# A state-space layer's first transform: half of the shift of its rows added by VectorE in the copy out of PSUM, and a new placing of the first stage's jobs and buffers

## The chip, the core and the metric

The kernel runs on one core of a Trainium2 chip. A core has five engines, each with its own queue of instructions that it takes in order: TensorE (PE in the profile; PEld is its weight load), VectorE (DVE), ScalarE (ACT), GpSimd (POOL) and SyncE (SP), which here only issues DMAs. TensorE writes PSUM; VectorE and ScalarE read and write PSUM and SBUF; GpSimd works on SBUF. The metric is the device time of one execution in microseconds.

## What is computed

A row of 2048 tokens with 640 channels passes a modulated layer norm, a long convolution whose filter comes from 192 complex modes per channel (an S4 layer), a second modulated layer norm and a bilinear gated unit.

```python
    mod = (_silu(c) @ w_mod).reshape(c.shape[0], 6, 1, -1)
    sa, ca, ga, sb, cb, gb = (mod[:, i] for i in range(6))
    h = _layernorm(x, axis=-1) * (1 + ca) + sa
    x = x + ga * _A_ref(h, ...)      # y = irfft(rfft(h) * rfft(K)) + h * Dskip
    h = _layernorm(x, axis=-1) * (1 + cb) + sb
    x = x + gb * _B_ref(h, ...)      # ((h @ w_gate) * (h @ w_up)) @ w_down
...
    P = jnp.exp(logdA[:, :, None] * l[None, None, :])
    K = jnp.einsum("dn,dnl,dn->dl", Cc, P, dB).real
```

## The kernel before, in words

The work falls into two stages. The **first stage** is the convolution. It takes the channels in five blocks of 128 (`db` 0 to 4). The **second stage** (the gated unit, from `u_head` on) is a fixed sequence of large matmuls.

The spine of the first stage is a loop of 40 filter steps (`n`, eight to a block), each in three parts (`t` = 3n, 3n+1, 3n+2). A step makes the modes' powers for 16 channels: GpSimd makes phases `Ph` and magnitudes `EQ` and `EP` as outer sums and products (line 729), ScalarE takes sines into PSUM tiles `tr`, VectorE multiplies them into `QtA`, `PtA`, `PtB`, `QtB` (lines 784, 785, 790, 810), and TensorE multiplies those into the filter `kg` (lines 825 and 840), which ScalarE copies to `Kt`.

All other work of the first stage consists of **jobs** that are hung between the parts of the steps:

- `u_seeds` (lines 524 to 680) prepares a block's modes, with exponentials on ScalarE; `tab_ph` makes tables on GpSimd.
- `u_stats` and `u_hm` normalise the input rows and store them to `hm` in DRAM; `u_modr`, `u_modc`, `u_modg` and `u_fold` compute the modulation (line 368 is its product), and `u_fold` leaves the shift of each channel, the same on every partition, in `shr`.
- `u_pre(db, q)`, 20 in all, is the first transform of the rows: it loads a tile `hf` from `hm`, multiplies it by the constants `t_s1h` (line 886) into two PSUM banks, `r[0]` for the real and `r[1]` for the imaginary half, adds the transform of the constant shift by a product of a constant row `t_one` with `shr` (one partition deep) into the same banks, and copies both banks to `hf` tiles, which are stored to `FH`.
- `u_k` transforms the filter (line 862), `u_g` and `u_c` do the second transform (line 907, constants `t_tw`), the product of the two spectra on VectorE (lines 946 to 956) and the inverse (line 967, constants `t_ti`), whose result `W` is stored to `WD` in DRAM; `u_d` loads `WD` into `TV` and the input rows into `xs`, does the last inverse product (line 988), adds the rows and stores `x2d`.

Each job is a generator that runs in pieces. The table `SCHED` gives every piece a number; the pieces whose number divided by ten is x are issued, in the order of their numbers, at the call `due(x)`, and there are two such calls in each part of a step. So the table alone sets the order on every engine's queue, those of the DMA issuers included. Tiles come from small **rings**: the table `SLOT` names for every allocation which buffer it takes (`hfa`, `hfb`, `hfc`, `xsa`, `xsb`, the PSUM banks `psfa`, `psfb`, `psfc`, and so on), and a tile waits until the last use of the one before it in that buffer.

At the end of the first stage `u_d` of block 4 gives the last columns of each row; `u_head` takes the row statistics, normalises, transposes and begins the gated unit. `warm` matmuls fill TensorE meanwhile.

Of the kernel before, what the change touches and what calls it, by code (L numbers as in the profile page):

```python
# [10 lines left out]
F32 = mybir.dt.float32  # L11
# [20 lines left out]
    ml=(47, -888, -934),  # L32
    mr=(((138, 140), (110, 111)), ((2, 74), (4, 83)), ((0, 27), (-862, 18))),
    st=(
        (48, 91),
        (69, 100),
        (71, 101),
        (-948, 5),
        (-1006, 0),
        (-965, 89),  # L40
        (-1010, -969),
        (-868, 34),
        (-938, -874),
        (-918, 0),
        (-1003, -929),
        (-947, -909),
        (-919, -868),
        (34, 63),
        (37, 69),
        (-912, 0),  # L50
    ),
    hm=(
        (10, 220),
        (302, 416),
        (-1002, 172),
        (-999, 389),
        (-1010, 182),
        (-961, 147),
        (59, 100),
        (123, 173),  # L60
        (246, 310),
        (290, 372),
        (162, 252),
        (121, 180),
        (210, 293),
        (297, 381),
        (391, 486),
        (473, 556),
    ),
    rstd=(124, 87),  # L70
    tab=(367, 828),
    fo=(162, 162, 208, 238),
    e0=(4, 158),
    ds=(483, 468, 275, 262),
    mc=((87, 192, 194, 200, 210), (153, 286, 303, 326, 337), (270, 359, 369)),
    q=(
# [4 lines left out]
    ),  # L81
    pre=(
# [5 lines left out]
    ),  # L88
    c=(
# [4 lines left out]
        (  # L94
            (2433, 2608, 2608, 2648, 2679, 2703),
            (2425, 2484, 2537, 2554, 2645, 2677),
            (2477, 2493, 2636, 2656, 2680, 2719),
            (2387, 2439, 2532, 2545, 2620, 2633),
# [8 lines left out]
    ),  # L107
    k=(
        (392, 464),
        (371, 384),  # L110
        (474, 512),
        (494, 503),
        (622, 637),
        (592, 599),
        (710, 710),
        (607, 639),
        (640, 677),
        (652, 660),
        (831, 865),
        (797, 803),  # L120
        (973, 990),
        (941, 961),
        (1060, 1060),
        (1060, 1060),
        (1125, 1152),
        (1353, 1363),
        (1274, 1275),
        (1390, 1425),
        (1482, 1495),
        (1506, 1519),  # L130
        (1576, 1590),
        (1524, 1542),
        (1757, 1758),
        (1791, 1791),
        (1747, 1747),
        (1720, 1720),
        (2005, 2019),
        (1893, 1909),
        (2048, 2049),
        (2020, 2031),  # L140
        (2083, 2095),
        (2218, 2252),
        (2287, 2298),
        (2350, 2355),
        (2328, 2328),
        (2344, 2352),
        (2461, 2497),
        (2497, 2510),
    ),
    low=(168, 419, 677, 899, 1101, 1385, 1631, 1857, 2075),  # L150
    w=(2478, 2613, 2684, 2668, 2879, 2879),
    wl=(2590, 2441),
    wm=(2732, 2755),
    h=(2709, 2738, 2775, 2811, 2843, 2843, 2857, 2875),
    g=(
# [5 lines left out]
    ),  # L161
)

SLOT = dict(
    Kt="abababbaabababbababa",
    Ph="ababababababababababbbabababababaaababbb",
    PtA="abababababababababababababababbabaababba",
    TV="baabababaabbaabbbabbaababbaababbaabbabbaababab",
    W="abbbbbabababbbbabbaabbaba",
    f16="abababa",  # L170
    gh="cbacbacbcacbacbacbbcbcacbabccaabcabacba",
    hf="abacbcabacbacabcbacccacaabbcbaacabaabbabcaccababbcbbacaabcabbcbba",
    psf="cacabccbcaccbabbaacbbcacabacbcbacacbbaacabbcabcabcbacbbcbcbcababccbacabcabacbacbaccacbacbaccababbcabcabcabbcabcabcacacab"
    "cbcbaacbacbacbabccabcaacabcaabcbcabcabccabcabcbbacbcbacbacbacbacbacbbabccabacbaacbcabcbacabcabcabcabcababcacbabcacbaacbc"
    "abaabcabcacbacbacacbacbacaaacacbcaba",
    tr="bbababababababababababababababababababababababbabbabababaababbaaababababababababababababababababbbabbababaababababbabbbb"
    "a",
    xs="aabababbabaaabababab",
)
SEG0 = ("l", "a", "b", "c", "ud", "r", "x", "e", "f", "G", "g", "", "h", "v", "R", "")  # L180
SEG = ("l", "a", "b", "c", "ud", "r", "R", "x", "eE", "f", "g", "h", "v", "D")
P_PH, P_EP, P_MOD = 3, 6, 1


def _tables():

    a = np.arange(32)
# [42 lines left out]
def tile_kernel(ctx: ExitStack, tc: tile.TileContext, I, out):  # L230
# [3 lines left out]
    def act(o, i, f=AF.Copy, **kw):  # L234
        return S.activation(o, i, f, **kw)  # L235
# [1656 lines left out]
```

## Time and profile before

| | us |
|---|---|
| median of three runs | 965.52 (962.56 to 967.35) |
| the profiled execution, its own time | 962.34 |
| its span, first to last instruction | 960.6 |

The profile shows that one execution. Busy time is the time in which an engine executed instructions; a row of a group gives an instruction's line, engine, operation, output and inputs with their shapes, the number of them, the busy time in us and the mean duration in ns, then the idle time of the engine just before and what ended it. A row of the timeline gives start and duration in us; in square brackets stands how long the engine sat idle and who released it. TensorE's records of one product are two, one for each pass. The last columns of a row by stretches are the granted clock of TensorE (1.00 is full speed), the busy share of the DMA engines and GB/s.

### The profile page before, as it was taken

To read this page: it belongs to the slowest core of one execution; us is meant where nothing else is said; L and a number is where in the kernel's file an instruction comes from. 1 tells how busy PE (TensorE), PEld (TensorE's weight loads), DVE (VectorE), ACT (ScalarE), POOL (GpSimd) and SP (SyncE) were. 2 spreads that over 40 slices of the span, in tenths; PEclk is the share of its full clock that TensorE was granted. 3 is DMA by queue.
4 is the path that set the end of the run, shared out by engine and by line. 5 is a ranking of instruction groups with operands and counts; after the bars stand their busy time and mean duration, and the time that the engine had idled before them with its cause. 6 is when DMAs were issued, how large, how long until landed. Compare 5 with 4: busy or idle time off the path is not lost.

```text
span 960.6 us, 27559 instructions
## 1 busy us (share of the span) xinstructions
PE 892.6 (93%) x11646; PEld 734.0 (76%) x11646; DVE 705.6 (73%) x1250; ACT 580.5 (60%) x1016; POOL 471.2 (49%) x369
## 2 busy tenths in 40 slices
PE   1898787999899899998889999999999999999998
PEld 1675555878776677887558888889999788888997
DVE  8977888878888986767688555557585766569952
ACT  6989999887988977763276333234463543435430
POOL 3998997986699668750041345320013323231110
PEclk9989999999999999999999999999999999999999
DMA  7876546435267646547894675435536576758875
GB/s 238 324 243 242 186 131 199 146 108 153 78 207 197 187 124 194 184 128 228 277 308 152 192 246 192 165 140 172 200 120 196 171 238 208 244 172 289 253 231 189
DMA packets 158819, 188.59 MB, mean 196 GB/s; under 512 B 9828, under 2 KB 128360, under 8 KB 157544
## 3 DMA queue, kind: packets, MB, share of 16 engines
q1 hardware_dynamic: 149480, 155.51, 50.3%
q0 software_dynamic: 4752, 21.63, 7.8%
q10 hardware_dynamic: 4464, 9.70, 2.7%
q8 instruction: 91, 1.49, 0.6%
q14 instruction: 32, 0.26, 0.1%
HBM read 124.22 MB, written 62.59 MB: 194 GB/s over the span
## 4 chain that ended last, share of the span: by engine, by line
PE 61%; ACT 12%; issue 10%; DVE 7%; POOL 5%; DMA 4%; SPq 0%; POOLq 0%; DVEq 0%; ACTq 0%
PE pa L1095 19%; PE psg L1095 9%; PE pa L1527 7%; PE kg L825 3%; PE kg L840 2%; PE psfa L907 2%; PE psfb L967 2%; PE psfb L907 2%; ACT L235 2%; PE psfc L967 1%; PE psfc L907 1%; PE psfa L967 1%; PE psfc L886 1%; ACT trb L235 1%; ACT tra L235 1%
## 5 line engine op out<-in xcount | busy, mean ns | idle before, releaser
L1072 POOL TENSOR_TENSOR tf<-wur,wgb 128x256 f32<-128x256 f32 x23 | 17.5, 760 | 241.5 <-DVE wtl L1043 193.2
L729 POOL TENSOR_TENSOR EQ<-LQ,RH 128x1536 f32<-128x1536 f32 x40 | 114.8, 2870 | 5.3 <-DVE QtB L785 5.3
L1043 DVE TENSOR_TENSOR wtl<-tf,wth 128x256 fp32r<-128x256 f32 (+1 forms) x72 | 37.0, 516 | 59.2 <-ACT wth L235 59.2
L729 POOL TENSOR_TENSOR Phb<-LH,DH 128x1536 int32<-128x1536 int32 x21 | 60.3, 2871 | 32.6 <-ACT trb L235 19.3
L729 POOL TENSOR_TENSOR EP<-LP,RH 128x768 f32<-128x768 f32 x40 | 61.9, 1547 | 1.7 <-ACT RH L235 1.7
L729 POOL TENSOR_TENSOR Pha<-LH,DH 128x1536 int32<-128x1536 int32 (+1 forms) x20 | 54.1, 2703 | 9.2 <-ACT trb L235 8.5
L1527 PE MATMUL pa<-wsg,sh 128*128 128x384 f32 (+1 forms) x304 | 58.1, 309 | 0.0
L840 PEld LDWEIGHTS kg<-QtB,PtB 64*32 64x32 f32 x2560 | 38.3, 108 | 13.4 <-issue 6.9
L1043 DVE TENSOR_TENSOR wsg<-wga,wsg 128x640 fp32r<-128x640 f32 x36 | 35.5, 988 | 14.8 <-ACT wsg L235 14.8
L840 PE MATMUL kg<-QtB,PtB 64*32 64x64 f32 x2560 | 44.6, 219 | 1.8 <-DVE QtB L785 1.8
L1527 PEld LDWEIGHTS pa<-wsg,sh 128*128 128x128 f32 x304 | 45.4, 188 | 0.0
L1566 POOL DMA_DIRECT2D wsg<-wdc x21 | 11.2, 532 | 66.6 <-PE pa L1579 35.7
L235 ACT ACTIVATE sh<-a 128x512 fp32r<-128x512 f32 x55 | 33.3, 626 | 13.9 <-PE psg L1579 6.2
L1043 DVE TENSOR_TENSOR sl<-a,sh 128x512 fp32r<-128x512 f32 x55 | 38.0, 710 | 3.9 <-ACT sh L235 3.9
L235 ACT ACTIVATE wsg<-wga 128x640 fp32r<-128x640 f32 x36 | 26.2, 731 | 23.7 <-PE pa L1527 12.6
L1095 PE MATMUL pa<-hh,wsg 128*128 128x512 f32 x150 | 40.0, 393 | 0.0
L235 ACT ACTIVATE a<-pa 128x512 f32<-128x512 f32 x12 | 7.2, 596 | 49.9 <-PE pa L1095 49.9
L235 ACT ACTIVATE s<-pa 128x512 f32<-128x512 f32 x12 | 7.2, 598 | 49.2 <-PE pa L1095 47.0
L235 ACT ACT_TABLE_LOAD x25 | 32.1, 1283 | 7.2 <-DMA pta<-A_A_re 4.2
L784 DVE TENSOR_TENSOR QtA<-trb,EQ 128x1024 f32<-128x1024 f32 x22 | 26.8, 1216 | 11.9 <-POOL EQ L729 4.4
L235 ACT ACTIVATE wth<-tf 128x256 fp32r<-128x256 f32 (+1 forms) x72 | 32.4, 481 | 4.5 <-DVE tf L1073 1.8
L1527 PE MATMUL pa<-wsg,sl 128*128 128x384 f32 (+1 forms) x152 | 34.5, 308 | 0.0
(672 smaller groups left out, 3230.0 us busy)
## 6 DMA issues: line engine op xcount, KB each, us to landing
wsg<-wdc POOLq DMA_DIRECT2D x21, 640.0 KB, 5.1
wgb<-B_w_gate SPq DMA_DIRECT2D x24, 320.0 KB, 4.1
wur<-B_w_up SPq DMA_DIRECT2D x24, 320.0 KB, 5.6
wsd<-wsg SPq DMA_DIRECT2D x12, 640.0 KB, 3.7
wga<-wdg SPq DMA_DIRECT2D x12, 640.0 KB, 3.9
wsg<-wsd POOLq DMA_DIRECT2D x12, 640.0 KB, 4.8
wdc<-xb SPq DMA_DIRECT2D x21, 320.0 KB, 4.5
TVb<-WD SPq DMA_DIRECT2D x26, 256.0 KB, 3.5
```

Of the source, the lines that this page charges most:

```text
L235: return S.activation(o, i, f, **kw)
L729: G.tensor_tensor(o.rearrange("p x (h l) -> p x h l", l=8), lo.unsqueeze(2).to_broadcast([P, rows, nh, 8]), hi.unsqueeze(3).to_broadcast([ ...
L784: return [lambda: V.tensor_tensor(Qt[:, :, :, 0:32], tr[:, :, :, ::-1], e[:, :, 0:32].unsqueeze(1).to_broadcast([P, 2, R, 32]), op=OP.mult ...
L825: PE.matmul(kg[j * 32 : j * 32 + 32, dd, :], PtA[:, c, dl * 4 + j, :], QtA[:, c, dl * 4 + j, :], start=dd == 0 and c == 0, stop=False, til ...
L840: PE.matmul(kg[j * 32 : j * 32 + 32, dd, :], PtB[lo : lo + 64, c, r, :], QtB[lo : lo + 64, c, r, :], start=False, stop=dd == 7 and c == 1, ...
L907: PE.matmul(r[c][par * 64 : par * 64 + 64, i, :], t_tw[:, k0 + k, c, :], src[:, k, :], start=True, stop=True, tile_position=(0, par * 64))
L967: PE.matmul(r[par][:, i], t_ti[lo : lo + 64, qd * 4 + i, c, :], y[lo : lo + 64, i, :], start=k == 0, stop=k == len(x) - 1, tile_position=( ...
L1043: V.tensor_tensor(lo, v, hi, op=OP.subtract)
L1072: E.tensor_tensor(t[:, 0:2], u[:, 0:2], g[:, 0:2], op=OP.subtract)
L1095: PE.matmul(ps, w[a][:, k], x[b][:, l], start=first and n == 0 and m == 0, stop=n == 2 and m == len(ks) - 1, skip_group_check=True)
L1527: PE.matmul(AC[tb][t][c], x[:, ts], w[:, cs], start=st, stop=f == NF - 1 and n == 2 and (c == 0 or t % 2 == 1))
L1566: G.dma_start(WD[q], wdc[:, q // 3, q % 3])
```

## The change

The real half of the shift is no longer a product. The constants lose the 64 columns for it and gain one column `t_on`, the real sums by partition; the matmuls with `shr` write `r[1]` alone; and where ScalarE copied `r[0]`, VectorE computes `shr * t_on + r[0]` into the same tile. The imaginary half keeps its product and its copy by ScalarE.

```diff
+    ones = np.tile(f.sum(1).T, (4, 1))
...
-    ct = kconst.tile([P, 800], F32, name="ct")
+    ct = kconst.tile([P, 737], F32, name="ct")
...
-    t_one = ct[:, 384:512].rearrange("p (c m) -> p c m", c=2)
-    t_s1k = ct[:, 512:768].rearrange("p (c k j) -> p c k j", c=2, j=4)
-    t_ib = ct[:, 768:800]
+    t_one = ct[:, 384:448]
+    t_on = ct[:, 448:449]
+    t_s1k = ct[:, 449:705].rearrange("p (c k j) -> p c k j", c=2, j=4)
+    t_ib = ct[:, 705:737]
...
-                for c in range(2):
+                for c in range(2) if i == 0 else (1,):
                     o = 64 * (j ^ c)
-                    PE.matmul(r[c][o : o + 64], (t_s1h, t_one)[i][a, c], h[a] if i == 0 else shr[a, d0].unsqueeze(1).to_broadcast([1, 4, P]),
-                              start=i == 0, stop=i == 1, tile_position=(64 * j, o))
+                    PE.matmul(r[c][o : o + 64], t_s1h[a, c] if i == 0 else t_one[a], h[a] if i == 0 else shr[a, d0].unsqueeze(1).to_broadcast([1, 4, P]),
+                              start=i == 0, stop=i == 1 or c == 0, tile_position=(64 * j, o))
         yield
         for c in range(2):
             Ft = ring(fp, [P, 4, P], "hf")
-            act(Ft, r[c])
+            if c == 0:
+                V.scalar_tensor_tensor(Ft, shr[:, d0].unsqueeze(1).to_broadcast([P, 4, P]), t_on, r[c], op0=OP.mult, op1=OP.add)
+            else:
+                act(Ft, r[c])
```

Beside it nearly every number of `SCHED` and letter of `SLOT` is another; of some 300 lines of them, three:

```diff
-    ml=(47, -888, -934),
+    ml=(38, 14, -923),
...
-        ((479, 551, 564), (291, 418, 427), (458, 503, 533), (606, 634, 652)),
+        ((431, 552, 563), (300, 405, 415), (259, 425, 470), (528, 609, 634)),
...
-    xs="aabababbabaaabababab",
+    xs="aabababbaabbabababab",
```

The lines of the changed file lie two to five higher, so line 886 is 888 there and 907 is 912. What the tables do to the queues is shown at three places. The first is the first `u_pre` on TensorE, in filter step 5; `ct` holds the constants, `hf` the rows. Before:

```order
L840 MATMUL kg<-QtB,PtB 32x64 x32
L862 MATMUL psfb<-ct,Kta 64x128 x8
L886 MATMUL psfa<-hfa,ct 64x512
L886 MATMUL psfc<-hfa,ct 64x512
L886 MATMUL psfa<-hfa,ct 64x512
L886 MATMUL psfc<-hfa,ct 64x512
L886 MATMUL psfa<-shr,ct 64x512
L886 MATMUL psfc<-shr,ct 64x512
L886 MATMUL psfa<-shr,ct 64x512
L886 MATMUL psfc<-shr,ct 64x512
L825 MATMUL kg<-QtA,PtAa 32x64 x32
```

With the change, on the same queue at the same step:

```order
L842 MATMUL kg<-QtB,PtB 32x64 x32
L864 MATMUL psfb<-ct,Kta 64x128 x8
L888 MATMUL psfc<-hfb,ct 64x512
L888 MATMUL psfa<-hfb,ct 64x512
L888 MATMUL psfc<-hfb,ct 64x512
L888 MATMUL psfa<-hfb,ct 64x512
L888 MATMUL psfa<-shr,ct 64x512 x2
L827 MATMUL kg<-QtA,PtAa 32x64 x32
```

Two of eight matmuls are gone, and bank `psfc` (`r[0]`) is complete after the data. Its eviction stood on ScalarE between two pairs of sines; it now stands on VectorE between two steps' products, here in the changed kernel:

```order
L792 TENSOR_TENSOR PtAa<-tra,EP_142 128x1024
L812 TENSOR_TENSOR PtB<-trb,EP_142 128x512
L786 TENSOR_TENSOR QtB<-trb,EQ_140 128x16x32
L787 TENSOR_TENSOR QtB<-trb,EQ_140 128x16x32
L894 SCALAR_TENSOR_TENSOR hfa<-shr,ct,psfc 128x512
L786 TENSOR_TENSOR QtA<-tra,EQ_141 128x32x32
L787 TENSOR_TENSOR QtA<-tra,EQ_141 128x32x32
```

What waits behind it are the products `QtA` of the next step. The second place is TensorE at the end of step 14. Before, the last four of 16 matmuls of a second transform (`f16` with `t_tw`) and a `u_k` stand there:

```order
L907 MATMUL psfb<-f16b,t_tw 64x128 x2
L907 MATMUL psfa<-f16b,t_tw 64x128 x2
L862 MATMUL psfc<-ct,Ktb 64x128 x8
L825 MATMUL kg<-QtA,PtAb 32x64 x32
L829 MATMUL kg<-dskt,ident 128x8
```

With the change the products of steps 14 and 15 follow each other:

```order
L972 MATMUL psfc<-ghb,t_ti 128x128
L842 MATMUL kg<-QtB,PtB 32x64 x32
L827 MATMUL kg<-QtA,PtAb 32x64 x32
L831 MATMUL kg<-dskt,ident 128x8
L912 MATMUL psfb<-gha,t_tw 64x128 x2
```

The job has moved behind step 15. The third place is SP's queue at the end of the first stage, where the loads of the last `u_d` of block 3 and the first of block 4 stand (`TV` from `WD`, `xs` from the input, stores to `x2d`, a load `wga` of the second stage's weights). Before:

```order
L980 DMA TVb<-WD 128x4x128 x2
L982 DMA xsb<-A_u 128x4x128
L980 DMA TVa<-WD 128x4x128 x2
L982 DMA xsa<-A_u 128x4x128
L1021 DMA wga_7266<-B_w_gate 128x5x256
L996 DMA x2d<-xsa 128x4x128
L996 DMA x2d<-xsb 128x4x128
L980 DMA TVb<-WD 128x4x128 x2
L982 DMA xsb<-A_u 128x4x128
```

With the change:

```order
L985 DMA TVb<-WD 128x4x128 x2
L987 DMA xsb<-A_u 128x4x128
L1001 DMA x2d<-xb_6937 128x4x128
L985 DMA TVa<-WD 128x4x128 x2
L987 DMA xsa<-A_u 128x4x128
L1026 DMA wga_7285<-B_w_gate 128x5x256
L1001 DMA x2d<-xsb 128x4x128
L1001 DMA x2d<-xsa 128x4x128
L985 DMA TVb<-WD 128x4x128 x2
```

A store of another `u_d` of block 3 (`xb`) now stands between the two pairs of loads, and the stores of `xsa` and `xsb` have changed places. That store's addition is the one that uses `xsb` before the first load here, and on VectorE it stands behind the whole spectral product of the stage:

```order
L958 TENSOR_TENSOR psfc<-psfc,f16a 128x256
L960 TENSOR_TENSOR f16a<-TVa,psfc 128x4x64
L961 TENSOR_TENSOR f16a<-TVa,psfc 128x4x64
L997 TENSOR_TENSOR xb_6937<-psfa,xsb 128x4x128
L1048 TENSOR_TENSOR wsg<-wga_7018,wsg 128x640 x2
L1000 TENSOR_TENSOR xsb<-psfb,xsb 128x512
```

Before, that addition stood ahead of seven such spectral products, and nothing between line 956 and the split of `wga`.

More of the change, by code (lines that the diff above doesn't have):

```diff
@@ L31 @@
 SCHED = dict(
-    ml=(47, -888, -934),
-    mr=(((138, 140), (110, 111)), ((2, 74), (4, 83)), ((0, 27), (-862, 18))),
-    st=(
[L35 to L50, printed above, removed]
-    ),
-    hm=(
[L53 to L68, printed above, removed]
-    ),
@@ L70 @@
[L70 to L75, printed above, removed]
-    q=(
[4 rows of a table removed]
+    ml=(38, 14, -923),
+    mr=(((103, 138), (85, 117)), ((35, 82), (23, 45)), ((-877, 33), (0, 56))),
+    st=(
+        (60, 115),
+        (40, 121),
+        (69, 127),
+        (-999, 8),
+        (-984, 3),
+        (-998, 109),
+        (-1010, -963),
+        (17, 37),
+        (-986, -888),
+        (1, 3),
+        (-998, -939),
+        (-983, -907),
+        (-883, 1),
+        (23, 67),
+        (36, 68),
+        (5, 5),
+    ),
@@ new lines @@
+    hm=(
+        (-889, 197),
+        (121, 398),
+        (-1010, 305),
+        (85, 399),
+        (-1010, 176),
+        (-1007, 270),
+        (77, 140),
+        (217, 273),
+        (39, 136),
+        (171, 232),
+        (172, 227),
+        (134, 181),
+        (294, 470),
+        (331, 369),
+        (402, 469),
+        (251, 445),
+    ),
+    rstd=(142, 86),
+    tab=(553, 739),
+    fo=(149, 149, 202, 228),
+    e0=(1, 159),
+    ds=(339, 378, 319, 440),
+    mc=((120, 175, 197, 201, 209), (192, 273, 273, 309, 317), (264, 369, 392)),
@@ L81 @@
+    q=(
[4 rows of a table added]
     ),
     pre=(
[5 rows of a table removed]
-    ),
-    c=(
[4 rows of a table removed]
-        (
[L95 to L98, printed above, removed]
[5 rows of a table added]
+    ),
+    c=(
[4 rows of a table added]
+        (
+            (2380, 2593, 2606, 2606, 2655, 2720),
+            (2446, 2513, 2534, 2567, 2634, 2656),
+            (2455, 2551, 2627, 2642, 2651, 2697),
+            (2431, 2453, 2513, 2566, 2623, 2623),
         ),
@@ L101 @@
     d=(
[5 rows of a table removed]
-    ),
-    k=(
[L109 to L148, printed above, removed]
-    ),
[L150 to L154, printed above, removed]
-    g=(
[5 rows of a table removed]
[5 rows of a table added]
+    ),
+    k=(
+        (402, 407),
+        (224, 230),
+        (454, 556),
+        (421, 426),
+        (484, 507),
+        (517, 548),
+        (639, 657),
+        (603, 603),
+        (706, 716),
+        (664, 680),
+        (777, 781),
+        (803, 804),
+        (1006, 1012),
+        (1029, 1037),
+        (1046, 1059),
+        (1046, 1075),
+        (1295, 1322),
+        (1120, 1137),
+        (1252, 1252),
+        (1388, 1406),
+        (1410, 1420),
+        (1505, 1522),
+        (1556, 1567),
+        (1481, 1509),
+        (1808, 1839),
+        (1737, 1774),
+        (1753, 1756),
+        (1784, 1785),
+        (1840, 1856),
+        (1883, 1912),
+        (1996, 2008),
+        (2063, 2073),
+        (2085, 2096),
+        (2141, 2191),
+        (2362, 2374),
+        (2274, 2274),
+        (2321, 2321),
+        (2447, 2455),
+        (2494, 2510),
+        (2452, 2466),
+    ),
+    low=(167, 428, 668, 910, 1139, 1389, 1628, 1864, 2075),
+    w=(2473, 2612, 2690, 2703, 2759, 2879),
+    wl=(2602, 2481),
+    wm=(2735, 2751),
+    h=(2562, 2755, 2793, 2818, 2854, 2858, 2862, 2876),
+    g=(
[5 rows of a table added]
     ),
@@ L164 @@
 SLOT = dict(
[L165 to L169, printed above, removed]
-    f16="abababa",
[L171 to L177, printed above, removed]
-    xs="aabababbabaaabababab",
+    Kt="ababababababbabbaaba",
+    Ph="abababababababababababababababababababbb",
+    PtA="babaababababababababababababababaaababab",
+    TV="ababababaabababbaabbababbaaabbabbbbabaabababab",
+    W="baaabbaaabbabaabaaabbbaba",
+    f16="abababa",
+    gh="bacbabcbcabacbacacbbabcabcabacbacabcabc",
+    hf="cbabcbabcacbaabccbcbaccbcababcacbccabaababcacbbaaaccabccbabaabbaa",
+    psf="bacbaacbaacccabbcabcbacbbbcabcbcaabacabbbcbcbcabcaaacbbcbcabcababccabcabcacbacbbabacbacabcbabacbabcabcbbacbacbacbaccacba"
+    "bacbcbcaabccbaaacbaccacabbccabacbacbabccabaacbcacbccbacabcaacbbacbacbaccaacbacbbababacbacbabcbabacbacbabcabacbacabcabcba"
+    "baabcababcbacbacbcbacbacbacacacbcabc",
+    tr="ababababababababababababababababababababababababababbabbababababababababababababababababababababbbabbabbababaabbabaababa"
+    "b",
+    xs="aabababbaabbabababab",
 )
@@ L224, in _tables @@
     t = {"t_tw": tw.reshape(128, 4096), "t_ti": ti.reshape(128, 4096),
-         "t_c": np.concatenate([perm, s1h.reshape(128, 128), one.reshape(128, 128), s1k.reshape(128, 256), ib.reshape(128, 32)], 1)}
+         "t_c": np.concatenate([perm, s1h.reshape(128, 128), one[:, 1].reshape(128, 64), ones[:, 0 : 1], s1k.reshape(128, 256), ib.reshape(128, 32)], 1)}
     return {k: np.ascontiguousarray(v, dtype=np.float32) for k, v in t.items()}
```

44 rows, old and new, of tables (c, d, g, pre) are left out of this document.

## The prediction

> **What bounds the kernel now.** I read the page's head and its chain first, then the busy time of each engine in stretches, then single rows. From the page:
>
> ```profile
> span 960.6 us, 27559 instructions
> PE 892.6 (93%) x11646; PEld 734.0 (76%) x11646; DVE 705.6 (73%) x1250; ACT 580.5 (60%) x1016; POOL 471.2 (49%) x369
> PE 61%; ACT 12%; issue 10%; DVE 7%; POOL 5%; DMA 4%; SPq 0%; POOLq 0%; DVEq 0%; ACTq 0%
> ```
>
> TensorE leads, but the other engines hold a third of the chain, and the stretches show where. The cuts below lie where the filter loop begins a multiple of five steps, then step 39, the head of the second stage, and the end; each column is the busy time of an engine in that stretch.
>
> ```profile
> core 0: us, PE busy (x) PEld busy (x) DVE busy (x) ACT busy (x) POOL busy (x), PEclk, DMA share, GB/s
> 34.00:86.00 52.00, 44.51 (x797) 34.93 (x795) 45.66 (x93) 46.89 (x79) 47.15 (x37) 0.93 0.77 264
> 86.00:133.00 47.00, 37.31 (x852) 25.11 (x854) 36.37 (x56) 46.26 (x77) 42.96 (x26) 0.93 0.59 192
> 133.00:184.00 51.00, 45.65 (x1071) 33.60 (x1065) 43.29 (x64) 46.69 (x78) 44.24 (x29) 0.97 0.48 147
> 184.00:231.00 47.00, 46.37 (x1186) 39.45 (x1184) 37.38 (x49) 37.95 (x67) 36.59 (x19) 1.00 0.47 144
> 231.00:288.00 57.00, 52.85 (x1220) 41.30 (x1220) 47.50 (x71) 48.94 (x83) 44.73 (x25) 1.00 0.50 148
> 288.00:338.00 50.00, 45.28 (x1058) 30.69 (x1050) 44.95 (x64) 46.08 (x77) 41.87 (x21) 0.97 0.66 186
> 338.00:389.00 51.00, 49.88 (x1177) 37.38 (x1170) 39.82 (x53) 38.12 (x68) 40.92 (x28) 1.00 0.58 171
> 389.00:431.00 42.00, 40.61 (x1034) 36.57 (x1035) 29.91 (x36) 29.58 (x52) 27.76 (x12) 1.00 0.45 144
> 431.00:492.00 61.00, 52.88 (x798) 38.31 (x793) 43.06 (x122) 21.53 (x42) 5.33 (x11) 1.00 0.83 255
> 492.00:960.00 468.00, 463.05 (x2444) 407.22 (x2442) 307.49 (x553) 195.24 (x372) 120.87 (x143) 1.00 0.62 203
> ```
>
> The last row is the second stage: TensorE works 463 of 468 us, and the change does not touch it, so it shifts as a block. Only the first 492 us can change. There, from 34 to 184, ScalarE is the fullest engine (46.89+46.26+46.69 = 139.8 of 150 us; GpSimd 134.4, TensorE 127.5, VectorE 125.3). From 184 on TensorE is the fullest or within 1 us of it (287.9 of 308 us).
>
> **The change, part by part.** *The removed matmuls.* A u_pre issues four data matmuls, then four with the shift row.
>
> ```profile
> 99.78 1.09 PE L862 MATMUL psfb<-ct,Kta 128*64 128x128 f32 x16 [0.26 <-DVE LQ L627]
> 100.81 0.64 PE L886 MATMUL psfa<-hfa,ct 64*64 64x512 f32 x1
> ...
> 101.83 0.64 PE L886 MATMUL psfa<-shr,ct 1*64 1x512 f32 x1
> ...
> 101.85 0.64 PE L886 MATMUL psfc<-shr,ct 1*64 1x512 f32 x1
> 102.31 0.59 PE L886 MATMUL psfa<-shr,ct 1*64 1x512 f32 x1
> ...
> 102.33 0.59 PE L886 MATMUL psfc<-shr,ct 1*64 1x512 f32 x1
> ```
>
> Each matmul is two records (a pass each). The four shift matmuls start within 0.02 us, because they sit in four different quarters of the array: from 101.83 to 102.92, 1.09 us for all. The change takes two of the four away; the two that stay have the same 512 columns and two passes. A row for two side by side is L862: eight matmuls of 128 columns in two column halves, 512 columns a half, also 1.09 us. So the saving is **0 us**. The other end is half of 1.09 us in each of 20 u_pre, -10.9 us; I take 0, by L862.
>
> *The evictions.* Twenty copies leave ScalarE and twenty scalar_tensor_tensor come to VectorE. The nearest rows:
>
> ```profile
> L235 ACT ACTIVATE hfa<-psfa 128x512 f32<-128x512 f32 x6 | 3.6, 594 | 2.6 <-PE psfb L886 2.6
> L948 DVE SCALAR_TENSOR_TENSOR ghb<-psfb,ghb 128x512 f32<-128x512 f32 x4 | 2.8, 692 | 0.4
> L634 DVE SCALAR_TENSOR_TENSOR prm<-ptb,dt,psfa x2: 415/415/415, 254.0 to 324.8; 128x192 f32<-128x192 f32 x2
> L635 DVE SCALAR_TENSOR_TENSOR psfa<-psfa,ptb x2: 366/366/367, 254.4 to 325.2; 128x192 f32<-128x192 f32 x2
> ```
>
> ScalarE loses 20 x 0.59 = 11.8 us. L948 is the new operation with a constant (0.692 us); L634 against L635 shows that a scalar per partition adds 0.05 us. VectorE gains 20 x 0.74 = 14.8 us. By the orders of before and of the change, eight u_pre stand ahead of step 15 in both; the other twelve come later. So in 34 to 184 ScalarE falls to 139.8 - 8 x 0.59 = 135.1, VectorE rises to 125.3 + 8 x 0.74 = 131.2, GpSimd keeps 134.4. ScalarE stays the fullest by a hair, and **-4.7 us** is what this stage can give; the other end is 0, if the wait below eats it. After 184 TensorE covers the other twelve: a shorter ScalarE is worth nothing while TensorE's queue is full, and if that cover were gone it would be 12 x 0.59 = 7.1 us.
>
> A rule of the Trainium skill speaks against the new operation. The trace shows it at work:
>
> ```profile
> 28.41 2.20 DVE L627 TENSOR_TENSOR LQ<-LQ,LQ 128x768 f32<-128x768 f32 x1
> 26.94 2.86 POOL L729 TENSOR_TENSOR EQ<-LQ,RH 128x1536 f32<-128x1536 f32 x1
> 29.76 3.54 POOL L729 TENSOR_TENSOR Phb<-LH,DH 128x1536 int32<-128x1536 int32 x1
> L627 DVE TENSOR_TENSOR LQ<-LQ,psfc 128x768 f32<-128x768 f32 x4 | 3.6, 946 | 0.0
> ```
>
> The product of two SBUF tiles took 2.20 us beside GpSimd's EQ, its like with one PSUM operand 0.946; the GpSimd operation behind it took 3.54 where EQ took 2.86. The new operation reads PSUM, a broadcast SBUF row and an SBUF scalar; L634 has just these kinds, at 0.415 us each time, so I take no such wait. The other end is 20 x (2.20 - 0.946) = 25 us on VectorE. The Trainium skill, "SBUF — State Buffer", section "SBUF: two separate sides", says that a Vector operation with two SBUF inputs and a GpSimd operation that reads SBUF exclude each other for a whole instruction. The trace agrees with L627; if the scalar counted as a second input the page would give the 25 us, and L634 speaks against it.
>
> *The new wait.* VectorE now waits for TensorE at 20 places, with the filter products QtA, PtA, PtB queued behind, for which TensorE's next step waits. Before, ScalarE waited there:
>
> ```profile
>   ACT hfa L235: 8.7, 6
>   ACT hfc L235: 2.0, 3
>   ACT hfb L235: 1.1, 2
> ```
>
> That is 11.8 us in 11 waits. The first bank is now complete about 1.0 us sooner (101.83 against 100.81, no second group), so most of these waits, of 1.1 us in the mean, shrink to nothing. I take 0; the other end is 11.8 us.
>
> *The moved jobs.* One stage-2 product (f16 with t_tw) that stood in step 14 comes after step 15, so 1.8 us of TensorE work slip from the stretch with room to that without. Its size:
>
> ```profile
> 440.36 0.44 PE L907 MATMUL psfb<-f16a,t_tw 128*64 128x128 f32 x4
> ...
> 442.15 0.28 PE L862 MATMUL psfa<-ct,Kta 128*64 128x128 f32 x2
> ```
>
> **+1.8 us**. The remaining moves keep the number of jobs in each stage within one or two; steps 30 to 34 lose a product, 35 to 38 gain one, both with TensorE full: 0. The load of the constants is shorter by 63 of 544 columns and lands long before its use: 0. The new ring letters change which older tile a new one waits for; a price for that I have only at the end of the stage, below. Early, the modulation products come sooner on TensorE. That touches a slow stretch:
>
> ```profile
> 53.80:57.20 3.40, 3.40 (x17) 3.40 (x16) 0.93 (x4) 3.37 (x5) 3.40 (x3) 0.50 0.67 202
> 57.20:60.60 3.40, 3.40 (x68) 2.71 (x68) 3.04 (x16) 2.96 (x5) 3.24 (x5) 0.57 0.91 267
> ```
>
> The granted clock is half there, with TensorE busy throughout: some 3 us are lost. Whether that stretch goes or another comes I cannot read from an order: 0, bounds -3 to +3.
>
> *The end of the first stage.* Here the queue of SP decides. The first addition for block 4 waits for an xs buffer that is stored and loaded again:
>
> ```profile
> 459.38 0.41 DVE L956 TENSOR_TENSOR f16a<-TVa,psfa 128x256 f32<-128x256 f32 x1
> 458.42 0.96 SPq L982 DMA_DIRECT2D xsb<-A_u  x1
> 474.75 0.37 SPq L982 DMA_DIRECT2D xsb<-A_u  x1
> 476.12 1.32 PE L988 MATMUL psfa<-TVb,ct 64*32 64x512 f32 x8
> 477.80 0.69 DVE L992 TENSOR_TENSOR xb<-psfa,xsb 128x512 f32<-128x512 f32 x1 [0.94 <-DMA xsb<-A_u]
> ```
>
> After the change the load at 458.42 must wait for one more addition (0.69 us), which now stands behind the operation at 459.38: its issue slips from 458.42 to about 460.5, and the loads behind it slip with it. In return that buffer's store no longer stands behind the other buffer's. TensorE's product ends at 477.44 anyway, 0.36 us before the addition starts. 0, bounds -0.4 to +2.
>
> **Sum**: -4.7 + 1.8 = -2.9 us. The profiled execution took 962.34 us (span 960.6), so 959.4 beside it. It lies 3.2 us under the median of the three runs, 965.52; on that footing the forecast is **962.6 us**.
>
> **The rivals.** (1) *The relief passes on in full.* ScalarE also leads, or nearly, from 231 to 338, and TensorE has 8.9 us free there (4.15 + 4.72). Six u_pre stand in it: 6 x 0.59 = 3.6 us more, and the slipped 1.8 us find room: -4.7 - 3.6 = -8.3, **957.2 us**. For it: 48.94 and 46.08 us of ScalarE; against it: VectorE, at 47.50 and 44.95, takes more than ScalarE gives. The Trainium skill, "TensorEngine Tiling (Array Packing)", section "PSUM Bottleneck", advises that both ScalarE and VectorE empty PSUM; by it this case would come about. (2) *The removed matmuls save time*, which needs the remaining pair to run in half the time: 962.6 - 10.9 = **951.7 us**; against it the row L862. (3) *VectorE becomes the bound*, slower. In 231 to 338 it has 92.45 us; six new operations with a wait of 1.07 each give 92.45 + 6 x 1.81 = 103.3, above TensorE's 98.1, +5.2. In 86 to 184 it has 79.66 + 8 x 1.81 = 94.1, above ScalarE's 92.95, +1.2. With the slipped 1.8: +8.2, **973.7 us**. It decides from the point where the new operations wait over 0.2 us each in the later stretch (98.1 - 92.45 - 4.4 = 1.2 us over six). For it: VectorE's 20 in-order waits; against it: the bank that is ready 1.0 us sooner. (4) *The port*: each new operation is longer by 1.25 us, 1.99 in all. Then 86 to 184 has 79.66 + 8 x 1.99 = 95.6 against ScalarE's 92.95, +2.6, and 231 to 338 has 92.45 + 6 x 1.99 = 104.4 against 98.1, +6.3; with the slipped 1.8, +10.7, **976.2 us**. Against it: L634.
>
> **How the numbers follow.** Forecast 0.47, rival 1 0.30, rival 2 0.04, rival 3 0.17, rival 4 0.02. About 0.5% (4.8 us) is what a measurement of this kernel can tell from no change. The forecast lies within it; rivals 1 and 2 are faster, 0.34; rivals 3 and 4 slower, 0.19. The forecast's own range is its open terms, -3 and +5 about 962.6 (the clock, the wait, the end): 959.6 to 967.6. The whole range reaches to rival 1 with the clock's 3 us more, and most of the way to rival 3: **953.5 to 972.0 us**.
>
> **What would show each step.** Right: eight records of shr to a u_pre become four and the pass still takes about 1.1 us; ScalarE's busy time falls by some 12 us and VectorE's grows by some 15; the stretch up to step 15 is 3 to 5 us shorter, and the head begins 2 to 4 us sooner; the second stage stays at 468 us. Wrong: VectorE's rows for the new operation show waits for TensorE of over 0.2 us in the mean, or durations over 0.8 us; the half-clock stretch is gone, or there are more; the load of xs lands more than 2 us later against the last product of the stage; the second stage changes its length.

## The result and the profile after

The change makes the kernel **slower**: 972.11 us (968.10 to 978.95, 13 runs) against 963.33 us (959.05 to 967.35, 13 runs), ratio 1.0093 with a 95% interval of 1.0074 to 1.0111, that is 9.0 us (7.1 to 10.7). The forecast was 962.6 us in 953.5 to 972.0, so the time lies outside the range by 0.1 us and on the side to which the forecast gave 0.19. The forecast was a sum of -2.9 us, set on a median of three runs, 965.52; the thirteen runs here have 963.33. So the sum is what to compare: -2.9 us was forecast, +9.0 us came.

From the page of the changed kernel (span, busy time by engine, and the chain that ended last, by engine):

```profile
span 967.5 us, 27413 instructions
...
PE 902.9 (93%) x11566; PEld 740.0 (76%) x11566; DVE 715.8 (74%) x1270; ACT 572.4 (59%) x996; POOL 471.3 (49%) x369
...
PE 63%; issue 8%; DVE 4%; ACT 4%; DMA 3%; POOL 1%; SPq 0%; POOLq 0%; DVEq 0%
```

The counts are as announced: 80 fewer records of TensorE, 20 fewer operations on ScalarE, 20 more on VectorE. The spans differ by 6.9 us. The same stretches as in the prediction, cut at the same filter steps (0, 5, 10, 15, 20, 25, 30, 35, 39, head, end); columns as there:

```profile
core 0: us, PE busy (x) PEld busy (x) DVE busy (x) ACT busy (x) POOL busy (x), PEclk, DMA share, GB/s
33.50:83.00 49.50, 44.00 (x806) 32.99 (x804) 45.41 (x94) 46.93 (x79) 46.39 (x37) 0.96 0.81 277
83.00:130.30 47.30, 41.19 (x758) 26.52 (x760) 37.50 (x55) 43.08 (x69) 44.07 (x27) 0.79 0.59 195
130.30:183.20 52.90, 47.45 (x1070) 34.77 (x1068) 46.88 (x68) 47.07 (x77) 42.97 (x28) 0.97 0.44 138
183.20:231.90 48.70, 46.94 (x1233) 40.09 (x1232) 42.14 (x60) 36.93 (x64) 45.63 (x23) 1.00 0.46 143
231.90:291.10 59.20, 54.67 (x1152) 41.74 (x1152) 48.32 (x74) 48.02 (x80) 40.93 (x23) 0.97 0.53 158
291.10:344.80 53.70, 46.03 (x1088) 32.84 (x1080) 46.58 (x67) 44.66 (x74) 38.78 (x20) 0.90 0.55 155
344.80:395.10 50.30, 48.51 (x1194) 38.46 (x1185) 40.66 (x54) 36.84 (x64) 45.45 (x29) 1.00 0.55 155
395.10:434.80 39.70, 39.64 (x993) 34.11 (x991) 31.18 (x37) 27.84 (x48) 23.27 (x11) 1.00 0.54 168
434.80:499.70 64.90, 56.97 (x825) 41.51 (x822) 44.07 (x124) 23.52 (x44) 5.52 (x11) 0.95 0.81 243
499.70:967.50 467.80, 463.01 (x2445) 407.21 (x2443) 304.08 (x552) 194.55 (x371) 120.62 (x143) 1.00 0.62 203
```

Up to step 15 the kernel is where it was before (183.2 against 184). Then it loses 1.7, 2.2 and 3.7 us in three stretches, wins back 3.0 us in the next two, and loses 3.9 us between step 39 and the head. The second stage is untouched, 467.80 us against 468.

The new operation itself (its line: durations, then what ended VectorE's idle time before it, in us and times, then who waited for it):

```profile
L894 DVE SCALAR_TENSOR_TENSOR hfb<-shr,ct,psfc x4: 737/738/739, 136.2 to 376.6; 128x512 f32<-128x512 f32 x4
...
  PE psfb L888: 1.9, 2
  PE psfc L888: 0.7, 1
...
  PEld kg L842: 1.6, 1
  ACT psfa L236: 1.3, 1
  PEld kg L827: 1.0, 2
  PE psfb L864: 0.9, 2
```

It takes 0.74 us and waits 2.6 us for TensorE in all. TensorE's products wait 0.9 us for it, and its weight loads, which overlap the products, 2.9 us. By these rows it is all but innocent. The experiments had to show whether that is so.

### The profile page after: what moved, and what is told of

Same layout as the page of the kernel before. It is cut to its first block, busy times and chain, and to the rows that moved or that the text cites. A ratio compares the mean times of both kernels' runs of the same rounds, so it can differ in the third digit from the quotient of the medians.

```text
span 967.5 us, 27413 instructions
## 1 busy us (share of the span) xinstructions
PE 902.9 (93%) x11566; PEld 740.0 (76%) x11566; DVE 715.8 (74%) x1270; ACT 572.4 (59%) x996; POOL 471.3 (49%) x369
## 4 chain that ended last, share of the span: by engine, by line
PE 63%; issue 8%; DVE 4%; ACT 4%; DMA 3%; POOL 1%; SPq 0%; POOLq 0%; DVEq 0%
PE pa L1100 19%; PE psg L1100 9%; PE pa L1532 7%; PE psfc L972 3%; PE psfb L972 3%; PE kg L842 3%; PE kg L827 2%; PE psfb L912 2%; PE psfa L912 2%; PE psfc L912 2%; PE psfb L888 1%; PE psfc L888 1%; PE psfa L864 1%; DMA TVa<-WD 1%; PE pa L1584 1%
## 5 line engine op out<-in xcount | busy, mean ns | idle before, releaser
L1048 DVE TENSOR_TENSOR wsg<-wga,wsg 128x640 fp32r<-128x640 f32 x36 | 33.4, 927 | 17.3 <-ACT wsg L236 17.3
```

Of the source, the lines that this page charges most:

```text
L1048: V.tensor_tensor(lo, v, hi, op=OP.subtract)
```

## The experiments

All ratios are to the kernel before, run beside it on the same chip. "Old placing" and "new placing" are the tables `SCHED` and `SLOT` of before and of the change.

### The code edit alone

The changed code with both tables of before:

```diff
-SCHED = dict(...)   # of the change
-SLOT = dict(...)
+SCHED = dict(...)   # of before
+SLOT = dict(...)
```

> The code edit alone: the matmuls of the real half of the shift removed and the copy moved to VectorE, with the placing tables of before. Theory A (the edit itself is harmless or helps, the new placing costs the 9 us): ratio to before 0.993 to 1.002, five or six half-clock stretches as before. Theory B (the edit costs, because VectorE's 20 in-order waits starve TensorE): ratio 1.006 to 1.012, VectorE's new operation waiting over 0.2 us in the mean. Theory C (the removed matmuls were activity that kept TensorE's clock up): ratio above 1.005 with more half-clock stretches than before and no long waits at the new operation.

Measured: **1.0239** (1.0212 to 1.0266), some 23 us. The ratio lies above the marks of theories A and B. Theory A is gone: the edit by itself costs more than the whole change, and together with the new placing the loss is 14 us smaller. Theory B had the reason wrong: VectorE never sat idle ahead of the new operation here. The marks of theory C are all met (sixteen half-clock pieces of 3.41 us in this profile, six before), so the next two runs must decide on it. What waits is TensorE. From its waits between 34 and 500 us (who waited, for whom; us, times, longest), those for the new operation:

```profile
PE psfc L912 <- DVE hfb L894: 5.3, 2, 2.8
...
PE psfb L972 <- DVE hfa L894: 3.6, 1, 3.6
...
PE psfa L972 <- DVE hfa L894: 2.2, 1, 2.2
...
PE psfb L864 <- DVE hfa L894: 1.9, 1, 1.9
PE psfb L912 <- DVE hfb L894: 1.9, 1, 1.9
PE psfb L912 <- DVE hfa L894: 1.8, 1, 1.8
PE psfc L912 <- DVE hfa L894: 1.7, 1, 1.7
...
PE psfb L972 <- DVE hfc L894: 1.2, 1, 1.2
...
PE psfc L537 <- DVE hfc L894: 0.6, 1, 0.6
```

Together 20.2 us in ten waits; the span of this profile is 27.3 us longer than before's. One of them in the timeline of this kernel:

```profile
148.38 0.59 PE L888 MATMUL psfb<-hfa,ct 64*64 64x512 f32 x1
...
148.62 0.68 DVE L786 TENSOR_TENSOR QtB<-tra,EQ 128x512 f32<-128x512 f32 x1
...
149.22 0.68 DVE L787 TENSOR_TENSOR QtB<-tra,EQ 128x512 f32<-128x512 f32 x1
149.82 1.22 DVE L786 TENSOR_TENSOR QtA<-trb,EQ 128x1024 f32<-128x1024 f32 x1
...
150.95 1.22 DVE L787 TENSOR_TENSOR QtA<-trb,EQ 128x1024 f32<-128x1024 f32 x1
...
152.08 0.74 DVE L894 SCALAR_TENSOR_TENSOR hfa<-shr,ct,psfb 128x512 f32<-128x512 f32 x1
...
152.87 0.48 PE L912 MATMUL psfb<-ghb,t_tw 128*64 128x128 f32 x2 [1.82 <-DVE hfa L894]
```

The bank `psfb` is full at 148.97. VectorE then has four products in its queue ahead of the new operation and empties the bank only at 152.08 to 152.82; TensorE's next product into `psfb` starts at 152.87, after 1.82 us without work. The same place before the change:

```profile
145.72 0.59 PE L886 MATMUL psfb<-shr,ct 1*64 1x512 f32 x1
...
146.37 0.60 ACT L235 ACTIVATE hfa<-psfb 128x512 f32<-128x512 f32 x1 [0.91 <-PE psfc L886]
...
147.30 0.44 PE L907 MATMUL psfb<-ghb,t_tw 128*64 128x128 f32 x4
```

ScalarE empties it 0.06 us after it is full. For all 20 tiles, from the end of the bank's last product to the start of its emptying: 0.38 us in the mean before (7.6 us in all), 2.58 us with the code alone (51.5 us), 1.08 us in the changed kernel (21.7 us).

### The matmuls alone

Before, with the product of the real half left out:

```diff
-                for c in range(2):
+                for c in range(2) if i == 0 else (1,):
...
-                              start=i == 0, stop=i == 1, tile_position=(64 * j, o))
+                              start=i == 0, stop=i == 1 or c == 0, tile_position=(64 * j, o))
```

> Before with only the shift matmuls of the real half left out; ScalarE copies both banks as before (the real half of the shift is missing from the output). Theory A: ratio 0.997 to 1.003, since the pair that stays takes as long as the four. If two of four matmuls take half the time: up to 10.9 us less, ratio 0.989. Theory C (activity): ratio above 1.004 with more half-clock stretches.

Measured: **0.9977** (0.9960 to 0.9993), 2.2 us less (0.7 to 3.9). Nearly nothing, as the prediction had it; not half of 20 x 1.09 us, and no harm from less activity.

### Their return under the new placing

The changed kernel with all four shift matmuls a tile, and a plain copy on VectorE:

```diff
-                V.scalar_tensor_tensor(Ft, shr[:, d0]..., t_on, r[c], op0=OP.mult, op1=OP.add)
+                V.tensor_copy(Ft, r[c])
...
-                for c in range(2) if i == 0 else (1,):
+                for c in range(2):
```

> The changed kernel with its placing, but the shift's real half is again a product into the bank, and VectorE only copies. Theory A (the removed matmuls are worth nothing either way): same ratio to before as the changed kernel, 1.007 to 1.011. Theory C (they kept the clock up): at least two half-clock stretches fewer than the changed kernel's, ratio 1.000 to 1.005. If four matmuls a tile cost TensorE more than two: ratio 1.012 to 1.020.

Measured: **1.0109** (1.0085 to 1.0133), not to be told from the changed kernel. One mark of theory C did come, eight half-clock pieces in this profile against the changed kernel's fourteen, but the time did not fall. With the run before it, in which the matmuls are gone and nothing is lost, theory C falls: the missing matmuls are not what the loss is made of.

### What of VectorE's operation costs: its time, the wait, or the bank

Three kernels that keep before as it is, ScalarE's copies included, and add one operation of VectorE at the place of the new one. They differ in one operand:

```diff
             act(Ft, r[c])
+            if c == 0:
+                V.bn_stats(pk1.tile([P, 2, 6], F32, name="st1")[:, 0, :], X)
```

X is the shift row (`shr[:, 0:512]`, which nobody waits for), then the bank `r[0]`, then ScalarE's copy `Ft`.

The shift row:

> Before, with ScalarE's copies as they are and one more VectorE operation at the place of the new one: statistics of 512 columns of the shift row, an estimated 0.6 to 0.7 us, into a scratch tile; no bank waits for it and nobody reads it. It adds VectorE's time and its place in the queue, but not the hold on the PSUM bank. If the 23 us of the edit under the old placing come from VectorE's time: ratio 1.015 to 1.024. If they come from the bank that is held until VectorE's turn: ratio 1.002 to 1.010.

Measured: **1.0007** (0.9990 to 1.0024). VectorE's 20 x 0.684 = 13.7 us are free.

The bank:

> Before, with ScalarE's copies and stores as they are; VectorE takes the statistics of bank r[0] into a scratch tile at the place of the new operation (0.68 us each, as in the run that read the shift row). Only the bank is now held until VectorE's turn. Theory of the held bank: the loss of the code alone comes back, ratio to before 1.012 to 1.024, with waits of TensorE for this operation of 10 us or more. Theory of the late store (what costs is that the copy itself, and the FH store and the loads behind it on SP, wait for VectorE): ratio 0.999 to 1.004.

Measured: **1.0307** (1.0276 to 1.0338), 29.6 us and more than the mark, although the copies and their stores are as early as before. Who waited for the operation:

```profile
  PE psfc L909: 8.3, 4
  PEld psfc L909: 5.7, 3
  PEld psfb L969: 5.0, 2
  PE psfb L969: 4.7, 2
  PEld psfb L909: 4.0, 2
  PE psfb L909: 3.6, 2
```

The copy:

> As the run that reads the bank, but VectorE reads ScalarE's copy hf in SBUF instead: VectorE waits for the product and ScalarE's copy, and holds the hf buffer, not the bank; one SBUF operand. Theory of the held bank: ratio 0.999 to 1.004. If VectorE's in-order wait for the product is the cost: 1.010 to 1.024.

Measured: **1.0033** (1.0014 to 1.0052). VectorE waits here in order for the product and for ScalarE, 5.0 us in four waits, the same as when it reads the bank, and that is worth 3 us. TensorE's products wait for the operation nowhere. So of the three suspects it is the **bank that stays taken until VectorE's turn**; the late store is not needed for the loss, and VectorE's time is none of it.

### The bank emptied by ScalarE, the shift added behind it

Code alone, with the copy by ScalarE and the addition in place:

```diff
+                act(Ft, r[c])
-                V.scalar_tensor_tensor(Ft, shr[:, d0]..., t_on, r[c], op0=OP.mult, op1=OP.add)
+                V.scalar_tensor_tensor(Ft, shr[:, d0]..., t_on, Ft, op0=OP.mult, op1=OP.add)
```

> The placing of before and the code of the change, but ScalarE copies the bank first, as before, and VectorE then adds the shift in place in SBUF: the same two matmuls gone, the same operation at the same place in VectorE's queue as in the run with the code alone (ratio 1.024), and only the PSUM bank is free without VectorE. Theory of the held bank: nearly all of the 23 us go, ratio to before 0.995 to 1.004. If VectorE's queue or its time were the cause: 1.015 to 1.025. If two SBUF operands make it collide with GpSimd (the 1.25 us a piece of the prediction's fourth rival): durations above 1 us and a ratio of 1.004 to 1.015.

Measured: **1.0244** (1.0212 to 1.0276). Read by itself this seemed to sink the theory of the bank; the rows of the operation tell why it does not (busy us, mean ns | idle before):

```profile
L895 DVE SCALAR_TENSOR_TENSOR hfb<-shr,ct,hfb 128x512 f32<-128x512 f32 x7 | 13.6, 1939 | 2.8 <-ACT hfb L236 2.8
...
L895 DVE SCALAR_TENSOR_TENSOR hfa<-shr,ct,hfa 128x512 f32<-128x512 f32 x8 | 10.7, 1331 | 0.6 <-ACT hfa L236 0.6
...
L895 DVE SCALAR_TENSOR_TENSOR hfc<-shr,ct,hfc 128x512 f32<-128x512 f32 x5 | 6.4, 1276 | 0.0
```

20 operations take 30.7 us instead of 14.8, up to 3.44 us for one. The timeline shows what holds them up: the longest runs from 207.21 to 210.65 and ends 0.55 us behind a product of GpSimd (207.25 to 210.10); the three that met no work of GpSimd took 0.74 us. TensorE's products wait nowhere for the new operation in this run, but 16.7 us between 34 and 500 us for VectorE's `QtB` and `PtA`, 6.8 us with the code alone. So the run most likely exchanged one cost for another, and it decides nothing on the bank; it is the price of the prediction's fourth rival, paid in another form of the operation.

### What is left under the new placing

The changed kernel with VectorE's addition done twice:

```diff
                 V.scalar_tensor_tensor(Ft, shr[:, d0]..., t_on, r[c], op0=OP.mult, op1=OP.add)
+                V.scalar_tensor_tensor(Ft, shr[:, d0]..., t_on, r[c], op0=OP.mult, op1=OP.add)
```

> The changed kernel with VectorE's addition done twice, the second over the first: 20 x 0.74 = 14.8 us of VectorE more, nothing else. If VectorE's time is what the change costs, the time grows by about as much as the change itself costs or more, 9 to 15 us, ratio to before 1.018 to 1.026. If VectorE has slack and only order and banks matter: ratio 1.009 to 1.013.

Measured: **1.0123** (1.0093 to 1.0153): 14.8 us of VectorE more, and each bank held 0.74 us longer, for 2.9 us, inside the measurement's spread. VectorE is not the bound.

The changed kernel with product and ScalarE's copy back for some tiles:

```diff
+ONACT = lambda db, q: db < 2 or db == 4 or (db, q) in ((3, 3), (2, 1))
...
-                for c in range(2) if i == 0 else (1,):
+                for c in range(2) if i == 0 or ONACT(db, q) else (1,):
...
-            if c == 0:
+            if c == 0 and not ONACT(db, q):
```

> The changed kernel's placing; in 14 of the 20 first transforms the real half of the shift is a product again and ScalarE copies, as before the change; the other six keep VectorE's addition. Theory B (VectorE's 20 operations are what the change costs, the new placing only hides part of it): 14 of 20 parts of the loss go, ratio to before 1.000 to 1.004. Theory A' (the new placing itself is the worse one, whoever evicts): ratio stays 1.008 to 1.012.

Measured: **1.0150** (1.0114 to 1.0187), above both marks. For the eight tiles of blocks 0 and 1 alone:

> As the run with 14, but only the eight tiles of blocks 0 and 1, which stand ahead of step 15, go back to ScalarE. Theory B with the loss spread evenly: ratio 1.004 to 1.007. If the loss is made behind step 15, where VectorE and TensorE are both nearly full: 1.008 to 1.010. If the early stage pays for it: 1.001 to 1.004.

Measured: **1.0105** (1.0086 to 1.0124). Neither brings anything back. With 14 tiles undone the kernel is slower than the change, with eight it cannot be told from it. The new placing with all 20 tiles on ScalarE, the direct measure of the placing, has no run.

In its place, the hold on the bank was taken away under both placings, with the same number of instructions in the same order on every engine; a fill of 0.49 us stands for the addition of 0.74 us, and the real half is left out of the output:

```diff
-                V.scalar_tensor_tensor(Ft, shr[:, d0]..., t_on, r[c], op0=OP.mult, op1=OP.add)
+                V.memset(Ft, 0.0)
```

> The changed kernel with VectorE's 20 operations replaced by filling the same tile with zeros (the real half of the first transform is left out of the output): the same number of instructions on every engine and the same order, but nothing on VectorE waits for the bank or holds it. If the held banks still cost under the new placing: 6 to 12 us less than the changed kernel, ratio to before 0.997 to 1.003. If what is left of the loss is the new placing itself: at most 3 us less, ratio 1.006 to 1.010.

Measured: **1.0099** (1.0072 to 1.0126).

> The same under the placing of before (the code alone, zeros in place of VectorE's operation; the real half of the first transform is left out of the output). Theory of the held bank: all of the 23 us go and ScalarE's 11.8 us and the two matmuls are saved besides, ratio to before 0.988 to 0.999. If another part of the code edit costs: above 1.005.

Measured: **1.0023** (1.0005 to 1.0041). The four corners, ratios to before:

| | VectorE empties the bank | nobody holds the bank |
|---|---|---|
| old placing | 1.0239 | 1.0023 |
| new placing | 1.0093 | 1.0099 |

Under the old placing the hold costs 1.0239 / 1.0023, some 21 us. Under the new one it costs nothing that can be measured (0.6 us less, with about 3 us of spread). The new placing itself costs 1.0099 / 1.0023, some 7 us, whoever empties the bank, and the code without the hold 2 us. Taken in this order they make the 9 us: 2.2 for the code, some 7 for the placing, nothing for the hold. Taken the other way, the hold comes first with 21 us and the new placing takes 14 of the 23 us away. The old placing without ScalarE's 11.8 us and without the two matmuls is no faster than before, so these 11.8 us are worth nothing here.

### Where the new placing loses

Mean lengths (us) from the timelines of five kernels of each placing, cut at the same steps; the last product is line 993 (988 before). For the old placing they are before, the one without the matmuls, the two whose extra operation reads the shift row or the copy, and the one that fills with zeros; for the new placing the change, the one with the matmuls back, the doubled addition, the one that fills with zeros and the first of the moved pieces below:

| | step 0 to 15 | 15 to 20 | 20 to 30 | 30 to 39 | 39 to the last product |
|---|---|---|---|---|---|
| old placing | 151.3 | 46.1 | 109.8 | 92.2 | 63.3 |
| new placing | 150.6 | 48.4 | 113.3 | 90.1 | 67.1 |

In two stretches the groups stand apart: 45.5 to 46.7 against 47.7 to 49.6 from step 15 to 20, and 62.6 to 64.1 against 66.0 to 68.6 behind step 39. In the others they overlap. From step 20 to 30 the old placing takes 107.3 to 108.1 in the three kernels that keep all shift matmuls, but 112.2 and 113.9 in the two without, against 112.7 to 114.2, so the 3.5 us there cannot be put down to the placing.

Three pieces of the new placing that the profile pointed to were moved, one at a time.

The addition of block 3 that held up a store and, behind it in SP's queue, the load of `TVa`:

```diff
-        ((2410, 2495, 2559), (2408, 2438, 2661), (2692, 2692, 2730), (2651, 2688, 2715)),
+        ((2410, 2495, 2559), (2408, 2438, 2600), (2692, 2692, 2730), (2651, 2688, 2715)),
```

> The changed kernel with one piece moved: the last addition of block 3 that uses the first xs buffer goes ahead of three spectral products of block 4, so that its store no longer holds up SP's load of TVa. If the profile's chain through that load is right, the last product of the stage and the head come 1.2 to 1.7 us sooner and the ratio to before falls to 1.007 or 1.008; if the load is late for another reason (the store of WD), nothing changes, 1.009.

Measured: **1.0119** (1.0090 to 1.0147), no gain. The load was issued 0.7 instead of 1.7 us behind the last spectral product of the stage, but TensorE's waits for it did not go. The changed kernel:

```profile
472.14 1.05 PE L993 MATMUL psfa<-TVa,ct 64*32 64x512 f32 x4 [0.46 <-DMA TVa<-WD]
474.71 1.78 PE L993 MATMUL psfa<-TVa,ct 64*32 64x512 f32 x4 [1.52 <-DMA TVa<-WD]
```

and with the addition moved:

```profile
473.15 1.05 PE L993 MATMUL psfa<-TVa,ct 64*32 64x512 f32 x4 [0.79 <-DMA TVa<-WD]
475.12 1.05 PE L993 MATMUL psfa<-TVa,ct 64*32 64x512 f32 x4 [0.93 <-DMA TVa<-WD]
```

From its issue to the start of the product's last part it is now 10.0 us (465.15 to 475.12) instead of 7.2 (467.48 to 474.71). With the earlier issue the load took longer, and the store of `xb` ahead of it in SP's queue is not what limits it; what does is not shown.

The filter transform that waits 4.0 us for VectorE in step 28 (in every kernel of the new placing, in none of the old):

```diff
-        (1737, 1774),
+        (1740, 1774),
```

> The changed kernel with one piece moved: the filter transform that waits some 4 us for VectorE's RH (bank psfa) in step 28 goes behind the products of that step instead of ahead of them. If that wait is part of the loss: 1 to 4 us less, ratio to before 1.005 to 1.008, and the stretch from step 25 to 30 falls from 53 to 50 or 51 us. If VectorE's queue sets the pace there anyway: no change, 1.009 to 1.011.

Measured: **1.0116** (1.0089 to 1.0142), and steps 25 to 30 still took 54.3 us. The wait itself stayed (3.5 us, now behind that step's products instead of ahead of them), so TensorE having work ahead of it or not is worth nothing there.

Three pieces of the seeds of block 4, as they stood before:

```diff
-        (1407, 1508, 1637, 1710, 1714, 1726, 1727, 1727, 1727, 1728, 1820, 1823, 1840, 1976),
+        (1407, 1508, 1637, 1710, 1714, 1726, 1727, 1748, 1748, 1748, 1820, 1823, 1840, 1976),
```

(with four letters of `psf` in the order that this makes)

> The changed kernel with three pieces of the seeds of block 4 placed as before the change: behind the products PtB and QtB of step 28 and not ahead of them. If the new placing loses because QtB, and GpSimd's EQ behind it, wait for VectorE's seed operations there: 2 to 4 us less, ratio 1.005 to 1.007, the stretch from step 25 to 30 down to 50 us and GpSimd's wait for QtB of 7.8 us gone. If that stretch is not where the loss is made: no change, 1.009 to 1.011.

Measured: **1.0171** (1.0145 to 1.0197); steps 25 to 30 grew to 62.3 us. Neither theory: the piece that looked misplaced was better where it was. Which of the placing's some 300 numbers make the 7 us stays **open**; only two stretches are known, with 2.3 and 3.8 us.

## Why the prediction was wrong

- **The step that failed is "the moved jobs", together with the gain of "the evictions".** The sum was -4.7 us for the early stage and +1.8 us for the moved jobs. The four corners measure the same terms: with no bank held, the code gives +2.2 us in place of -4.7, and the new placing costs some 7 us in place of +1.8. The moved jobs were sized by counting jobs in each stage, and the new ring letters had a price only at the end; a placing also sets the order of the queues and the buffers, and nothing in the sum stood for that.
- **Of those 7 us** the slipped stage-2 product came about as worked out: steps 15 to 20 are 2.3 us longer, and in the changed kernel the products of `f16` with `t_tw` take 7.9 us there instead of 6.3. Of the 3.8 us behind step 39, about 2 are a filter transform and a part of a second transform (0.9 us each) that steps 30 to 39 no longer do. The rest of the 3.8 us stays open: TensorE's waits for the loads of `TVa` are 2.0 us there in both profiles, and the changed kernel has two half-clock pieces in that stretch where before has none. What else makes the 7 us is not known.
- **"The new wait" was taken as 0 and came out so, but not by its reasoning.** The prediction asked how long VectorE would wait for TensorE at 20 places, and that was right: 2.6 us in all. It did not ask how long a full bank waits for its turn in VectorE's queue, and who needs that bank next. It even named what stands in that queue, but as waiting behind the new operation, not as standing ahead of it. Under the old placing that is 2.58 us a tile instead of 0.38, and 21 us in the end. Under the new placing it is 1.08 us, and it costs nothing that can be measured. That the zero held is luck of the placing, which the prediction priced as a separate term.
- **The early stage** was to give 4.7 us through ScalarE; it gave 0.5 (149.7 us from step 0 to 15 against 150.2). Its lower end, 0, was right. With ScalarE freed, the matmuls gone and no bank held, the old placing still took 1.0023: ScalarE was the fullest engine of that stage, at 139.8 of 150 us, and not what set its pace.
- **The removed matmuls** were taken at 0 with an end at -10.9 us; measured -2.2 us. The row of line 862 was the right one to read.
- **The operation's duration** was 0.74 us as estimated, and it never met GpSimd, as the row of line 634 said it would not.
- **The second stage** shifted as a block, 467.8 us.
- **The third rival** gave 973.7 us, 1.6 us from the measured time, by a mechanism that is not at work: VectorE did not become the bound (13.7 us more of its time cost nothing before the change, 14.8 us more cost 2.9 us after it) and its operation waits 0.13 us in the mean, below the 0.2 us that the rival needed. A number that fits is no proof of its reason.
- **The granted clock** was left at 0 with 3 us to either side. In this profile 23.9 us of full clock are missing against 10.2 before, 13.7 more. The mean granted clock of a run has a median of 0.977 (13 runs) against 0.984 (79 runs of before beside the experiments). At the same clock, 0.979 to 0.9825, before has a median of 964.5 us (29 runs) and the changed kernel one of 969.4 us (5 runs). So about 5 of the 9 us are there at equal clock, and the rest goes with a lower clock. Why the clock is lower is not shown: from step 0 to 15, where 13.7 us of full clock are missing against 8.5, TensorE sat idle for 17.1 us, less than the 22.5 before.

## What to carry to other kernels

When an eviction moves to another engine, look at three times, not two: what the operation costs, how long its engine waits for the product, and how long the full bank waits for that engine's turn. The last is read from the queue of the new engine (what stands ahead of the operation when the product ends) and counts whenever the next product into that bank is near. A hold can also cost nothing under another order of the queues, as here; then it does not appear in the list of waits. A new placing is a change of its own: here it cost some 7 us by itself, which counting the jobs of each stage did not show, so price it by a run that leaves the rest of the change out.

## What the runs showed of the hardware

The half clock comes in pieces of 3.41 us on a fixed grid, and two gaps of TensorE, of 1.71 and 3.02 us, were met by three of them. The changed kernel around step 5, in windows of that grid:

```profile
78.96:82.37 3.41, 2.29 (x72) 2.12 (x72) 3.39 (x5) 3.34 (x8) 3.41 (x2) 1.00 0.96 297
82.37:85.78 3.41, 1.13 (x34) 0.96 (x38) 2.84 (x5) 3.37 (x5) 3.41 (x3) 0.50 0.26 99
85.78:89.20 3.42, 3.42 (x53) 2.71 (x46) 3.32 (x7) 3.39 (x5) 3.21 (x2) 0.50 0.40 114
89.20:92.61 3.41, 3.41 (x8) 2.23 (x7) 1.02 (x3) 3.36 (x4) 3.41 (x3) 0.50 0.74 254
92.61:96.02 3.41, 3.41 (x14) 2.38 (x14) 1.83 (x2) 3.34 (x7) 1.88 (x3) 1.00 0.00 0
```

Each piece costs up to half its length, 1.7 us; the profile of before has six of them, that of the change fourteen. The Trainium skill, "TensorE: Matmul & The Clock Gate", section "What's actually happening", gives a free-running window of 3413 ns, with which the grid agrees, and full speed after one busy window; here the window from 85.78, busy throughout, was followed by another at half speed.

A run's time follows this clock: of before's 79 runs those at 0.987 or more (17) have a median of 961.7 us, those at 0.978 or less (8) one of 965.3 us.

An operation of VectorE with one PSUM operand, one SBUF operand and a scalar per partition from SBUF took 0.73 to 0.75 us in all 40 cases of the code alone and the changed kernel, 36 of them beside work of GpSimd; with the PSUM operand in SBUF instead, 0.74 to 3.44 us. So the scalar per partition does not make it collide with GpSimd, and the second tile does. This is what the Trainium skill says of two SBUF inputs in "SBUF — State Buffer", section "SBUF: two separate sides"; the trace adds that the scalar does not count.
